# Entry 0's queries in one load: three chunks of a fused attention and feed-forward kernel are loaded and turned together

## The chip, the cores and the metric

The kernel runs on one core of a Trainium2 chip. The metric is device time in microseconds (us) of one execution; several executions are timed and their median is given. A separate execution was taken by the hardware profiler, and all durations below are from that one.

The core has five engines with a queue each: PE multiplies matrices and writes to PSUM, ACT evaluates functions and copies, DVE does elementwise work, POOL does elementwise work and issues most of the loads, SP issues the stores and the transposing transfers. Each works in its own order and waits for the others through semaphores. 16 DMA engines move the data.

## The reference

Eight batch entries, eight heads, 576 tokens, head size 64. Attention has no softmax: the scores are scaled, multiplied by a decay that depends on the distance of the two tokens, and multiplied with the values. The result, heads side by side, goes through a feed-forward layer with 512 inputs and 2048 hidden units.

```python
scores = scale * np.matmul(q, k.transpose(0, 1, 3, 2))
gamma = 1.0 - 2.0 ** (-5.0 - np.arange(H))
rel = pos[:, None] - pos[None, :]
Dmat = np.where(rel >= 0, gamma[:, None, None] ** rel[None, :, :], 0.0)
attn_out = np.matmul(scores * Dmat[None], v)
x = attn_out.transpose(0, 2, 1, 3).reshape(B * S, H * D)
h = x @ w_in
out = (h * (1.0 / (1.0 + np.exp(-1.702 * h)))) @ w_out
```

## The kernel before

**Two halves on one PE queue.** The attention makes `xT`, the input of the feed-forward layer with the 512 features on partitions and tokens along the row. The feed-forward layer takes 512 tokens at a time: `hidden` (L732) multiplies `w_in` with `xT` and ACT puts the result through the activation into `gT`; `project` (L765) multiplies `gT` with `w_out`. The attention of the entries 1 to 7 is cut into 21 bursts (L587) that are placed between the products of the feed-forward layer. Only entry 0 has no such products to lie between: the first feed-forward products need its 384 first tokens. Its attention is written out by hand, from L852 on, and is called the front here.

**The front, chunk by chunk.** Entry 0 has five chunks, four of 128 tokens and one of 64. For a chunk n of the first four, the steps are

- `transposes` (L405): PE turns the chunk's queries and keys, four products of 128x128 each with the identity matrix, so that the head dimension comes onto the partitions. They go to a PSUM bank, and `evac_t` (L416) copies queries and keys in one ACT instruction of 128x1024 to `qk`.
- `intra` (L537): eight products make the scores (L431) in two PSUM banks, and DVE multiplies them with the mask (L441) into `sm`.
- `values` (L444): eight products with the values (L454); eight that add to a running state of keys and values (L467); from chunk 1 on, eight that multiply the chunk's queries with the state of the chunks before it (L482).
- `evac_z` (L503): ACT copies the state to `zq` for the next chunk. `evac_o` (L514): DVE multiplies the outputs with the query's decay into `xT`.

Between these steps `fill` (L828) issues products of zeros, 23 in all, which nobody reads. After the outputs of chunk 2 the first four `hidden_part` (L838) start with the columns 0 to 384, and chunk 3 is finished among them. From there on PE has feed-forward products.

**PSUM.** There are eight banks: `S` is two banks for scores, `O` and `Z` one each for outputs and state, `W` one for turned operands, `H0`, `H1` and `U` the three of `psB`. The scores of chunk 1 use `H0` and `H1` (`intra(1, 1)`), those of the chunks 0, 2 and 3 use `S`. Each bank (or pair) has a key, and an instruction of another engine on the same key waits.

**Loads.** Queries and values of chunk 0 come by SP in 32-bit form and are converted by DVE. All other loads are issued by POOL in the order of the code (L808 to L824) and are converted to bf16 on the way. A load of a chunk (L219) has eight heads by 128 tokens, 1024 packets, each 64 numbers. Its packets carry 256 B in memory and 128 B in the on-chip buffer. Before chunk 3's queries and keys come those of the chunks 1 and 2 and their values. POOL then issues two quarter-loads of `w_in` (512 packets of 512 B written), and multiplies the values of the chunks 1 and 2 with their factors (L390) before it issues the remaining loads. From the 23rd of these loads on (weights not counted), `pace` (L206) lets a load wait for the sixth before it.

The order of instructions is that of the calls; a recorder (`Rec`) keeps for each key who wrote and read it and makes the waits. The buffer `st_q` has three slots of five chunks; entry 0 uses slot 0, entry 2 is the first to use slot 2.

## Time and profile before

| | |
|---|---|
| median of 3 runs | 300.31 us (299.10 to 302.96) |
| the profiled execution | 298.93 us, of it 297.1 us from the first to the last instruction |
| PE busy | 291.1 us, 98% of the span |
| ACT, DVE, POOL busy | 125.9, 123.1, 151.6 us |
| first feed-forward product of the front (L843) | 17.12 us after the span's start |

The span is counted from the first instruction; all times of single instructions are counted from there too. A row of the timeline gives an instruction's start, its duration (for several in a row, from the first start to the last end), its engine, line and operands, how many there are, and in brackets the idle time of the engine before it with what ended it. PE overlaps its products, so the time that eight products take from PE is the distance to the next start, not the sum of their durations.

### The profile page before, as it was taken

The page shows a single profiled execution, that of the slowest core. Times are in us where ns is not written, and L with a number is a line of the kernel's source. Part 1 is how long each engine was busy: PE and PEld are TensorE (multiplying, and loading weights), DVE is VectorE, ACT ScalarE, POOL GpSimd, SP SyncE. Part 2 cuts the span into 40 slices and gives each one's busy share as a digit, 9 for nine tenths or more (in the row PEclk, how much of TensorE's full clock was granted, in tenths as well). Part 3 has the DMA queues.
Part 4 walks back from the last instruction along what each step waited for, and adds up shares of the span by engine and source line. Part 5 has one row for each costly group of instructions (what it writes and reads, how often), then busy time and mean ns, then how long its engine had stood idle before and what let it go on. Part 6 is the DMA issues. An engine that isn't in the chain of part 4 may idle for free.

```text
span 297.1 us, 7697 instructions
## 1 busy us (share of the span) xinstructions
PE 291.1 (98%) x3399; PEld 148.5 (50%) x3399; DVE 123.1 (41%) x221; ACT 125.9 (42%) x208; POOL 151.6 (51%) x205
## 2 busy tenths in 40 slices
PE   7799999999999999999999999999999999999996
PEld 3464455848544444544454445545454445444444
DVE  7769475454445435532615324245326504000012
ACT  6658426617256313540355045503660275026600
POOL 8975979989959887568984797000000000000000
PEclk9999999999999999999999999999999999999999
DMA  9999999999999999999999999904820200030012
GB/s 133 156 186 190 173 171 165 188 131 140 182 140 143 183 143 175 194 130 134 154 218 124 114 188 162 85 2 108 170 38 2 107 37 2 0 108 35 0 50 93
DMA packets 154850, 36.04 MB, mean 121 GB/s; under 512 B 145472, under 2 KB 150336, under 8 KB 154816
## 3 DMA queue, kind: packets, MB, share of 16 engines
q0 software_dynamic: 116304, 18.10, 94.1%
q1 hardware_dynamic: 38512, 17.44, 32.6%
q8 instruction: 27, 0.44, 0.6%
q14 instruction: 7, 0.06, 0.1%
HBM read 36.70 MB, written 9.44 MB: 155 GB/s over the span
## 4 chain that ended last, share of the span: by engine, by line
PE 94%; POOL 2%; DMA 2%; issue 0%; DVE 0%; POOLq 0%
PE psB L765 40%; PE psB L732 36%; PE psB L749 5%; PE psA L627 2%; DMA st_k<-in_k_dram 2%; PE psA L599 2%; PE psA L641 2%; PE psA L615 1%; PE psA L765 1%; PE psA L791 1%; PE psB L843 1%; PE psA L411 1%; POOL st_k L219 1%; POOL st_q L219 1%; POOL st_v L219 1%
## 5 line engine op out<-in xcount | busy, mean ns | idle before, releaser
L765 PE MATMUL psB<-w_out_sb,gT 128*128 128x512 bf16 x544 | 122.0, 380 | 0.0
L732 PE MATMUL psB<-xT,w_in_sb 128*128 128x512 bf16 x492 | 108.9, 379 | 0.0
L737 ACT ACTIVATE gT<-psB 128x512 bf16<-128x512 f32 x123 | 73.5, 597 | 38.4 <-PE psB L732 38.1
L765 PEld LDWEIGHTS psB<-w_out_sb,gT 128*128 128x128 bf16 x544 | 51.8, 98 | 60.2 <-DVE sm L696 0.3
L732 PEld LDWEIGHTS psB<-xT,w_in_sb 128*128 128x128 bf16 x492 | 47.5, 98 | 56.5
L685 DVE TENSOR_TENSOR xT<-psA,gq 128x768 bf16<-128x768 f32 x21 | 20.1, 958 | 115.3 <-PE psA L615 115.3
L232 POOL DMA_DIRECT2D st_k<-in_k_dram x70 | 52.5, 774 | 15.2 <-DMA st_k<-in_k_dram 10.9
L774 ACT ACTIVATE osb<-psB 128x512 f32<-128x512 f32 x31 | 18.5, 597 | 90.2 <-PE psB L765 86.8
L232 POOL DMA_DIRECT2D st_v<-in_v_dram x70 | 51.9, 767 | 5.7 <-DMA st_v<-in_v_dram 3.3
L219 POOL DMA_DIRECT2D st_q<-in_q_dram x39 | 34.8, 891 | 10.2 <-DMA st_q<-in_q_dram 7.6
L390 DVE TENSOR_TENSOR st_v<-st_v,vfac 128x512 bf16<-128x512 bf16 x36 | 23.3, 681 | 1.2 <-DMA st_v<-in_v_dram 1.2
L714 DVE TENSOR_TENSOR zacc<-zacc,psA 128x256 f32<-128x256 f32 x49 | 20.5, 419 | 6.9 <-PE psA L627 5.7
L696 DVE TENSOR_TENSOR sm<-psA,maskw 128x768 bf16<-128x768 f32 x21 | 19.9, 948 | 0.0
L749 PE MATMUL psB<-xT,w_in_sb 128*128 128x256 bf16 x128 | 15.0, 273 | 0.0
L777 DVE COPY osb<-psB 128x512 f32<-128x512 f32 x3 | 2.1, 692 | 29.7 <-PE psB L765 29.7
L749 PEld LDWEIGHTS psB<-xT,w_in_sb 128*128 128x128 bf16 x128 | 12.2, 98 | 1.7
L418 ACT ACTIVATE qk<-psA 128x1024 bf16<-128x1024 bf16 x8 | 8.2, 1022 | 9.8 <-PE psA L411 9.8
L599 PE MATMUL psA<-sm,st_v 64*64 64x64 bf16 x504 | 11.8, 195 | 0.3
L627 PE MATMUL psA<-st_v,st_k 64*64 64x64 bf16 x448 | 11.8, 199 | 0.0
L627 PEld LDWEIGHTS psA<-st_v,st_k 64*64 64x64 bf16 x448 | 7.5, 105 | 8.3 <-issue 7.8
L755 ACT ACTIVATE gT<-psB 128x512 bf16<-128x512 f32 x16 | 9.4, 599 | 5.0 <-PE psB L749 5.0
L615 PE MATMUL psA<-qk,zw 64*64 64x64 bf16 x448 | 11.1, 194 | 0.0
(103 smaller groups left out, 164.3 us busy)
## 6 DMA issues: line engine op xcount, KB each, us to landing
out_dram<-osb SPq DMA_DIRECT2D x35, 256.0 KB, 3.9
st_q<-in_q_dram POOLq DMA_DIRECT2D x31, 128.0 KB, 7.5
st_k<-in_k_dram POOLq DMA_DIRECT2D x57, 64.0 KB, 7.3
st_v<-in_v_dram POOLq DMA_DIRECT2D x57, 64.0 KB, 7.0
w_out_sb<-in_moe_w_out_dram POOLq DMA_DIRECT2D x4, 512.0 KB, 10.9
w_in_sb<-in_moe_w_in_dram POOLq DMA_DIRECT2D x3, 512.0 KB, 8.6
st_k<-in_k_dram POOLq DMA_DIRECT2D x4, 128.0 KB, 4.8
w_in_sb<-in_moe_w_in_dram POOLq DMA_DIRECT2D x2, 256.0 KB, 6.8
```

The source lines that it names most:

```text
L219: paced(R.op("POOL", lambda e, d=d, s=s: e.dma_start(d, s), w=[(nm, sl, c)], dma=(nm, sl, c), own=pace()))
L232: paced(R.op("POOL", lambda e: [e.dma_start(d, s) for d, s in parts], w=[(nm, sl, c)], dma=(nm, sl, c), parts=2, own=pace()))
L390: R.op(eng, lambda e: e.tensor_tensor(t, t, f, ALU.mult), r=[("vfac", min(b, 1))], w=[("v", sl, c)])
L627: i = e.matmul(psA[half(j), bank, off + 64 * t : off + 64 * t + 64], rows_of(st_k, m_in, g, u, h), rows_of(st_v, m_in, g, u, h), start=(t ...
L685: R.op("DVE", lambda e: e.tensor_tensor(xT[:, :, t0 : t0 + 192].rearrange("p (u j) n -> p u j n", u=2), psA[:, 2:4, 0:384].rearrange("p u ...
L696: R.op("DVE", lambda e: e.tensor_tensor(o, i, k, ALU.mult), r=["maskw"], w=[("sm", si(m))], ps=["S"])
L714: R.op("DVE", lambda e, to=to, src=src, was=was: e.tensor_tensor(to, was, src, ALU.add), r=[("zacc", (blk - 1) % 3)], w=[("zacc", blk)], p ...
L732: i = e.matmul(bank, w_in_sb[:, a, 128 * f : 128 * f + 128], xT[:, a, 512 * c : 512 * c + 512], start=(a == 0), stop=(a == 3))
L737: R.op("ACT", lambda e: e.activation(gT[c % 2][:, f, :], bank, AF.Gelu_apprx_sigmoid), w=[("gT", c % 2, f)], ps=[key])
L749: m = e.matmul(bank[:, 256 * i : 256 * i + 256], w_in_sb[:, a, 128 * (f + i) : 128 * (f + i) + 128], xT[:, a, a0 : a0 + 256], start=(a == ...
L765: i = e.matmul(bank, gT[c % 2][:, f, 128 * r : 128 * r + 128], w_out_sb[:, f, :], start=(f == 0), stop=(f == NF - 1))
L774: R.op("ACT", lambda e: e.activation(osb[m].ap(), bank, AF.Copy), w=[("osb", m)], ps=[key])
```

## The change

The queries of entry 0's chunks 1 to 3 are 384 tokens. They are loaded in one transfer `load_q4` in place of three. A partition takes four tokens that follow one another, and 96 partitions hold a head's 384. Four tokens of a head are 1024 B without a gap in memory, so that the load has 768 packets of 512 B written, where the three had 3072 of 128 B. They are put in slot 2 of `st_q`.

In this form a chunk's tokens are not on partitions of their own. PE turns all three chunks at once in `turn_q4`: for every pair of heads, every one of the four token positions and each head of the pair a product of 96 partitions by 64 columns with the 96x96 identity matrix, 32 products. They fill the banks `H0` and `H1`. `evac_q4(n)` copies the chunk n's queries from there to `qk`, 128x512 by ACT, and reads with a step of 96 numbers between neighbours so that the tokens come out in order. The keys of the chunks 1 to 3 are turned on their own (`turn_k`), four products and a copy of 128x512 each.

Since `H0` and `H1` are taken, the scores of chunk 1 go to `S`, and those of chunk 2 to `H0` and `H1`, after the copy of chunk 3's queries has left these banks. The outputs of chunk 2 are made and scaled ahead of chunk 3's scores, as before, without the products of zeros in between; 19 of the 23 products of zeros stay. POOL issues the values of chunk 3 and the second half-load of `w_in` ahead of its two multiplications. The threshold of `pace` is lowered by two, as there are two loads fewer.

```diff
+        q4 = st_q[0:96, 2, 0:4, :].rearrange("p c x -> p (c x)").rearrange("p (h x) -> p h x", h=H)
+        def load_q4():
+            s = q[0, :, 128:512, :].rearrange("h (p j) d -> p h (j d)", j=4)
+            paced(R.op("POOL", lambda e: e.dma_start(q4, s), w=q4_keys, dma=("q4",), own=pace()))
...
+        def turn_k(n, at=None):
...
+                for hp in range(HP):
+                    i = e.matmul(to[:, a, hp, :], t[:, sl, c, 128 * hp : 128 * hp + 128],
+                                 ident.ap(), is_transpose=True)
...
+            R.op("ACT", lambda e: e.activation(qk[n % NQK][:, a, :, :], to[:, a, :, :], AF.Copy),
+                 w=[("qk", n % NQK, a)], ps=[key])
...
+        psQ_keys = [("H", 0), ("H", 1)]
+        def turn_q4():
+            def fn(e):
+                for hp in range(HP):
+                    for j in range(4):
+                        for hh in range(2):
+                            i = e.matmul(psQ[half(hh), hp, 96 * j : 96 * j + 96],
+                                         q4[:, 2 * hp + hh, 64 * j : 64 * j + 64],
+                                         ident[0:96, 0:96], is_transpose=True)
+                return i
+            R.op("PE", fn, r=["ident"] + q4_keys, ps=psQ_keys)
+        def evac_q4(n, eng="ACT"):
+            i = psQ[:, :, 0:384].rearrange("p h (j t) -> p h t j", j=4)[:, :, 32 * n - 32 : 32 * n, :]
+            o = qk[n % NQK][:, 0, :, :].rearrange("p h (t j) -> p h t j", j=4)
+            if eng == "ACT":
+                R.op("ACT", lambda e: e.activation(o, i, AF.Copy), w=[("qk", n % NQK, 0)], ps=psQ_keys)
...
-        load(0, 1, "qk")
-        load(0, 2, "qk")
+        load(0, 1, "k")
+        load_q4()
+        load(0, 2, "k")
         load(0, 1, "v")
         load(0, 2, "v")
-        load(0, 3, "qk")
+        load(0, 3, "k")
         load_w_in(0, 1)
         load_w_in(1, 2)
+        load(0, 3, "v")
+        load_w_in(2, 4)
         scale_v(1, "POOL")
         scale_v(2, "POOL")
-        load(0, 3, "v")
-        load_w_in(2, 4)
...
         transposes(0)
         evac_t(0)
-        later_gq(2)
         constants_mask3()
         fill(4)
-        transposes(1, second)
-        evac_t(1, second)
+        turn_k(1, second)
+        later_gq(2)
         intra(0)
-        fill(4)
-        intra(1, 1)
-        transposes(2)
-        evac_t(2)
+        fill(2, (psV[:, 0, :], "O"))
+        turn_q4()
+        evac_q4(1)
         values(0, third[0])
+        turn_k(2)
+        evac_q4(2)
+        intra(1, 0)
         evac_z(0)
+        evac_q4(3)
         evac_o(0, third[0])
         later_gq(3)
         fill(2, second)
-        intra(2)
+        intra(2, 1)
         values(1, third[1])
         evac_z(1)
         evac_o(1, third[1])
-        fill(1)
-        transposes(3)
-        evac_t(3)
+        turn_k(3)
         values(2, third[0])
         evac_z(2)
         evac_o(2, third[0])
-        fill(1)
         gelu_table()
         intra(3)
```

## The prediction, made before the changed kernel ran

> **What bounds the kernel now.** First the page's busy times, then the chain of work that ended last in order of time, then who waited for whom, then the timeline of the first 20 us by engine. The page:
>
> ```profile
> PE 291.1 (98%) x3399; PEld 148.5 (50%) x3399; DVE 123.1 (41%) x221; ACT 125.9 (42%) x208; POOL 151.6 (51%) x205
> ```
>
> PE is busy for 291.1 of 297.1 us. The list of waits, for PE alone over the whole span, has three lines:
>
> ```profile
> PE psA L411 <- DMA st_k<-in_k_dram: 1.3, 1, 1.3
> PE psB L831 <- DVE lnh L270: 1.2, 1, 1.2
> PE psA L411 <- DVE mask L307: 0.3, 1, 0.3
> ```
>
> All three lie in the front. The busy share flatters the front, since fills count as busy; but from 17.12 us on PE has feed-forward products and the same query over 35 to 297 us shows no wait. The change touches nothing behind the front: the sequence of instructions of every engine is the same there. So the kernel gets faster or slower by what the first feed-forward product (L843) moves. The chain of work, cut to the front:
>
> ```profile
> 7.93 0.81 POOL st_q L219
> 8.74 6.04 DMA st_k<-in_k_dram
> 14.78 0.14 issue
> 14.91 0.61 PE psA L411 x8
> 15.52 0.34 PE psA L454 x8
> 15.87 0.12 PE psA L467 x8
> 15.99 0.36 PE psA L482 x8
> 16.35 0.02 issue
> 16.37 0.70 DVE xT L518
> 17.08 0.05 issue
> 17.12 2.12 PE psB L843 x12
> ```
>
> Read it from below: 17.12 is set by chunk 2's outputs (DVE 16.37 to 17.07), these by PE's work on chunk 2, and that stood in PE's queue behind the turning of chunk 3, which waited for chunk 3's keys: issued at 8.74, landed at 14.78, 6.04 us later. The other seven such loads of 1024 packets ahead of it took 4.5 to 4.7 us from issue to landing (k0 excepted, which met the early loads). Asked for this load alone, the source view gives 4.7/5.4/6.0 for a window that also has the queries before it: 6.0 is the exception.
>
> **The change, part by part.** I replay the front with durations of rows. Those that carry it:
>
> ```profile
> 10.32 0.40 PE L411 MATMUL psA<-ident,st_q 128*128 128x128 bf16 x4
> 10.55 0.39 PE L411 MATMUL psA<-ident,st_k 128*128 128x128 bf16 x4
> 10.87 0.41 PE L454 MATMUL psA<-sm,st_v 128*64 128x128 bf16 x8
> 11.12 0.29 PE L467 MATMUL psA<-st_v,st_k 128*64 128x64 bf16 x8
> ```
>
> From start to start: four turning products 0.22, eight products with values 0.25, eight for the state 0.23; further, by the same timeline, eight scores 0.34, eight inter-chunk products 0.34, a fill 0.216. A copy on ACT starts 0.2 after the end of its products; a DVE step starts 0.44 after the first of eight score products; after ACT or DVE, PE follows in 0.06. DVE masks in 1.23 and scales outputs in 0.68, 0.1 of it overlapped with the next.
>
> *When the new load lands.* Now k1 is issued at 3.55; with no q1 before it, at 2.65, and the new load at 3.55. Not shown: a load of 768 packets of 512 B by 96 partitions. Lower end: it takes what a small load takes, 4.5, and lands at 8.05. Upper end: the first quarter of `w_in`, packets of the same size, 6.6 after issue, so 10.15. For the value: between 6 and 10 us, 4668 small packets pass (1167 per us, 0.88 us a load); between 13 and 14.9 us, 655 packets of 512 B (345 per us), 2.2 us for 768; the two `w_in` quarters land 1.25 us apart (9.61 + 6.6 and 10.35 + 7.1), 1.9 us for 768. So 1.0 to 1.35 longer than a small load: it lands at **9.3** (9.05 to 9.4). The Trainium skill (DMA: Bandwidth & Descriptors, section Anatomy of one DMA) fits a load issued by POOL as 2.0 us plus its bytes at 436 GB/s; for 0.79 MB that is an estimate of 3.8 us, and the load would be there at 7.35, before PE is free for it; the sum would be the -0.8 of the third rival below. For a small load of 0.26 MB the same fit gives 2.6 against the 4.5 that all rows show, so I go by the rows.
>
> *The 32 products.* Not shown either. Lower end 0.031 us each: the products with values also write halves of 64 partitions in turn and take 0.25 for eight. Upper end 0.043: 0.055 of a full turning product by 96/128 columns, with no overlap of the halves. Taken: the middle, 0.037, 1.2 us. 9.35 to 10.55. PE is free from 9.0 (fill 6.99 to 7.86, turning of k1 0.22, scores(0) at 8.27 after the copy that ends at 8.21, two fills 0.43), so nothing of this is hidden: queued behind it are outputs(0), the turning of k2 and scores(1).
>
> *The copies.* Three ACT copies of 128x1024 go (1.02 each), six of 128x512 come. Contiguous, those take 0.60 (the activation L849, 128x512), 0.51 from start to start. With a step of 96 numbers in PSUM no row exists: lower end 0.51, upper end 0.92 as for 1024 numbers. Taken: 0.51, the nearest row by size. ACT: q1 10.75; k2 at 11.45 (PE: outputs(0) 10.55, state 10.8, turning k2 11.03 to 11.25); q2 11.96; `evac_z(0)` 12.47 (0.28); q3 12.75 to 13.35.
>
> *The bank.* scores(2) now wait for the copy of q3 to leave `H0` and `H1`: 13.41 instead of 12.06. This is the added wait. Queued behind it on PE: outputs(1), the turning of k3, outputs(2). Mask(1), 11.86 to 13.1, and outputs(0) on DVE end before mask(2) is due at 13.85, so DVE is not late. mask(2) ends at 15.08, outputs(2) begin at 15.15, their inter products at 15.63, DVE scales 16.08 to 16.77, and the first feed-forward product starts at **16.83** against 17.12.
>
> *The wait that goes.* k3's turn comes at 14.57, after outputs(1), and costs 0.22 ahead of outputs(2), which wait for mask(2) until 15.15 anyway. k3 is issued at 7.05 instead of 8.74, behind equal bytes; at the pace above it lands at 12.9, with the extra 1.5 of before at 14.4. So this wait is covered by 0.2 to 0.5 us even with a late piece; beyond 14.9 it would cost one for one. What is late next is the chain load, products, copies, bank.
>
> *POOL and the rest.* Two issues fewer are 1.75 us. The values' factors are applied from 11.2 on (they stood at 11.10), end 13.4, and are wanted at 13.75 and 15.15: nothing. v3 and `w_in` ahead of them go out 3.5 us earlier, but behind a busy DMA; `w_in` is wanted at 16.8, where its first quarter (16.2 before) is there. Four fills fewer (0.86) and 0.53 net on the turning products cost PE nothing that is on the path. Late loads, SP's queue and the pacing stay in step.
>
> Sum: 16.83 - 17.12 = -0.3 us. On the profiled execution 298.93 that is 298.6. The runs' median, 300.31, lies 1.4 above the profiled one, so the time to be expected of a median is 300.31 - 0.3 = **300.0**.
>
> **The rivals.**
>
> *The chain through the new load is longer* (slower than before). Place: load, products, six copies, bank. It decides against the change when the first feed-forward product passes 17.12, that is when the load lands after 9.6, or the strided copies take over 0.65 from start to start (the first has 0.19 of slack before the copy of k2 is due at 11.45, the second and third stand on the path in full). Price: at the upper ends, landing at 10.15 gives +0.85, copies of 0.92 give 0.22 + 0.41 + 0.41 = +1.0, products at 0.043 +0.2, together 2.05 above the forecast; a piece as late as k3's was, 1.5 in place of the 0.85, makes 2.7. That is 300.3 to 302.7, middle 301.3. For it: the slow landings of k3 and `w_in`. Against: the seven loads near the new place in time were all regular.
>
> *The clock.* PE's first eleven fills, 1.19 to 6.07, take 0.44 each; the four at 6.99 take 0.26 and less: PE starts at half speed. The change takes four fills away, and turning products take a larger part of PE's work: place, the stretch from 9 to 17 us; it decides once a stretch is too poor in other products. Between 13.6 and 17.0 us PE was busy for 2.08 of 3.4 us and the products at 17.12 still took 0.18 each (2.12 for twelve), so what was there was enough. If the front falls back to half speed for as long as at the start, 4.9 us, 2.4 us of work are lost: 302.4. The Trainium skill (TensorE: Matmul & The Clock Gate, Part 4) says that turning products do not count as work for the clock, which speaks against this change; by that rule the least busy stretch before would already have been poor, and the trace shows no fall.
>
> *The wait was the whole story* (more gain). If the load lands by 9.0, when PE is free (its lower end is 8.05), and the products take 0.031, every step behind comes 0.5 earlier and the first feed-forward product is at 16.35: -0.8, 299.5. Nothing above gives more, as the rest of the chain stays.
>
> *It does not do what it says:* k3 still comes late and PE waits for it again. With k3 at 16.0 the gain is gone and 0.8 lost: 301.1. The chain would name its load.
>
> **How the numbers follow.** Forecast (16.4 to 17.2): 0.6. Longer chain 0.22, clock 0.06, more gain 0.08, k3 late 0.04. All of these move the time by under 1%, less than the runs' own spread of 3.9 us around it, so the range is set by both: from 299.5 less 1.2 (the lowest run lies 1.2 under the median) to the longer chain's end at 302.7: 298.3 to 302.7, which leaves out an unlucky median. A change of 2%, 6 us, about what can be told from no change here, needs more than any rival gives: 0.02 faster, 0.03 slower.
>
> **What would show it.** The row of the 32 products: start (9.3) and distance to outputs(0) (1.2). The three strided copies' mean: 0.6 or more. PE's wait ahead of scores(2), on ACT, and DVE's mask(2) at 13.85. No wait of PE on `st_k`; instead one on the new load of `st_q`. First L843 product at 16.8, each 0.18. I am wrong if that product starts later than 17.2, or if the time moves without it.

## The result

| | kernel before | changed kernel |
|---|---|---|
| median | 299.99 us (299.10 to 302.96, 6 runs) | 303.80 us (302.99 to 304.78, 6 runs) |
| ratio | | 1.0118 [1.0068, 1.0167] |
| profiled execution | 298.93 us, span 297.1 | 303.15 us, span 301.4 |
| first feed-forward product of the front | 17.12 us | 17.99 us |

A second set of runs of the changed kernel gave 303.61 us against 299.70, ratio 1.0137 [1.0085, 1.0188]. The predicted time was 300.0 and the range ended at 302.7: the kernel is 3.8 us slower, and both signs of error that the prediction had named came true. The front is late, by 0.87 us instead of 0.3 us early; and the end moved by 4.3 us, so in this execution most of the loss arises behind the front. (Ratios leave out executions more than 1.5% above the fastest of their kernel; where a loss comes and goes from one execution to the next, as it will below, the median of all runs is therefore given beside the ratio.)

The page of the changed kernel, its line of busy times and one of its groups of instructions (the group's last column is the idle time of the engine just before these instructions and what ended it):

```profile
PE 290.5 (96%) x3415; PEld 147.7 (49%) x3415; DVE 123.0 (41%) x221; ACT 126.3 (42%) x211; POOL 150.4 (50%) x203
L775 PE MATMUL psB<-xT,w_in_sb 128*128 128x512 bf16 x492 | 109.1, 380 | 2.1 <-issue 2.1
```

PE has 3415 products, 16 more than before, and is busy for 0.6 us less, in a span that is 4.3 us longer: it stands still more. The second line is the feed-forward layer's `hidden` (L732 before), 2.1 us idle ahead of it with the releaser "issue", that is, nothing the profile shows. The list of waits, for PE alone over the whole span, with the first six of its eleven lines (total, times, longest):

```profile
PE psB L775 <- issue: 2.1, 1, 2.1
PE psB L437 <- DMA st_k<-in_k_dram: 1.3, 1, 1.3
PE psB L875 <- DVE lnh L277: 1.2, 1, 1.2
PE psB L474 <- ACT qk L463: 1.0, 1, 1.0
PE psB L453 <- DMA st_q<-in_q_dram: 0.8, 1, 0.8
PE psB L887 <- DVE xT L561: 0.5, 1, 0.5
```

Before, there were three lines, all in the front, and none behind it. Here the 2.1 us on "issue" are one single pause. The timeline of PE shows where:

```profile
95.60 0.28 PE L658 MATMUL psA<-qk,zw 64*64 64x64 bf16 x12
95.82 1.25 PE L775 MATMUL psB<-xT,w_in_sb 128*128 128x512 bf16 x5
99.14 1.04 PE L775 MATMUL psB<-xT,w_in_sb 128*128 128x512 bf16 x4 [2.07 <-issue]
```

Five large products after a group of small ones (the attention of a later entry, 96 products in 0.96 us), PE stops in the middle of a row of identical products whose operands are all there, and goes on 2.07 us later. The fifth large product starts at 96.69 and the sixth at 99.14, where 0.22 apart is usual. That is 2.2 of the 4.3 us; the front gives 0.9, and the rest comes in three steps of 0.4 to 0.7 us between 37 and 90 us, two of them with a short wait on "issue" (0.28 us up to 79.1 and 0.17 us up to 89.4).

The chain of work that ended last, cut to the front (start, duration, what), answers the prediction's replay:

```profile
2.73 0.82 POOL st_k L219
3.55 7.44 DMA st_q<-in_q_dram
10.99 0.04 issue
11.04 0.87 PE psB L453 x32
11.91 0.23 PE psA L497 x8
12.13 0.12 PE psA L510 x8
12.26 0.34 PE psA L437 x4
12.60 0.02 issue
12.62 0.60 ACT qk L441
13.22 0.49 ACT qk L463
13.71 0.28 ACT zq L548
13.98 0.50 ACT qk L463
14.48 0.05 issue
14.53 0.42 PE psB L474 x8
...
15.04 1.24 DVE sm L484
16.28 0.04 issue
16.32 0.41 PE psA L497 x8
...
17.25 0.70 DVE xT L561
17.95 0.04 issue
17.99 1.15 PE psB L887 x6
```

It is the predicted chain, link by link: load, products, copies, bank, mask, outputs, scaling. It starts 1.7 us late, since the new load took 7.44 us and landed at 10.99 instead of 9.3. From landing to the first feed-forward product it takes 7.0 us; the prediction had 7.5.

A last view: the issues of transfers between 2 and 18 us, with the median time to landing in the last column. First the kernel before, then the changed one:

```profile
w_in_sb<-in_moe_w_in_dram POOLq DMA_DIRECT2D x2, 256.0 KB, 6.8
st_v<-in_v_dram POOLq DMA_DIRECT2D x3, 128.0 KB, 4.7
```

```profile
w_in_sb<-in_moe_w_in_dram POOLq DMA_DIRECT2D x2, 256.0 KB, 8.2
st_q<-in_q_dram POOLq DMA_DIRECT2D x1, 384.0 KB, 7.4
st_v<-in_v_dram POOLq DMA_DIRECT2D x3, 128.0 KB, 7.5
```

The loads of the values are the same instructions in both kernels, and issued earlier in the second; yet they take 7.5 us at the median instead of 4.7. So the new load is not only late itself, its neighbours are late with it. Each load lands in 16 pieces. In the trace of the changed kernel, chunk 1's keys, issued at 2.65, ahead of the new load, have 15 pieces by 6.61 and the last at 8.96; the new load itself has 14 by 9.31 and the last two at 10.71 and 10.99.

### The profile page after: what moved, and what is told of

Its sections match the earlier page's. It is cut to its first block, busy times and chain, and to the rows that moved or that the text cites. A ratio compares the mean times of both kernels' runs of the same rounds, so it can differ in the third digit from the quotient of the medians.

```text
span 301.4 us, 7729 instructions
## 1 busy us (share of the span) xinstructions
PE 290.5 (96%) x3415; PEld 147.7 (49%) x3415; DVE 123.0 (41%) x221; ACT 126.3 (42%) x211; POOL 150.4 (50%) x203
## 4 chain that ended last, share of the span: by engine, by line
PE 91%; DVE 3%; DMA 2%; issue 1%; POOL 1%; ACT 1%; POOLq 0%; DVEq 0%
PE psB L808 38%; PE psB L775 36%; PE psB L792 5%; DMA st_q<-in_q_dram 2%; PE psA L670 2%; PE psA L642 2%; PE psA L684 1%; PE psA L658 1%; PE psA L834 1%; PE psB L887 1%; PE psA L808 1%; POOL st_k L219 1%; PE psA L418 1%; DVE gT L344 1%; DVE sm L484 0%
## 5 line engine op out<-in xcount | busy, mean ns | idle before, releaser
L817 ACT ACTIVATE osb<-psB 128x512 f32<-128x512 f32 x31 | 18.5, 597 | 90.3 <-PE psB L808 89.8
L219 POOL DMA_DIRECT2D st_q<-in_q_dram x36 | 32.8, 910 | 10.5 <-DMA st_q<-in_q_dram 7.1
L642 PEld LDWEIGHTS psA<-sm,st_v 64*64 64x64 bf16 x504 | 7.8, 107 | 2.5 <-issue 1.7
```

The costliest lines, as they stand in the source:

```text
L219: paced(R.op("POOL", lambda e, d=d, s=s: e.dma_start(d, s), w=[(nm, sl, c)], dma=(nm, sl, c), own=pace()))
L642: i = e.matmul(psA[half(t), 2 + u, at : at + 64], rows_of(st_v, m_out, g, u, 4 * u + 2 * t + j), smw[si(m_out)][half(r), j, 2 * blk + t, : ...
```

## The experiments

Two questions were to be told apart: what the pause at the 97th us is, and what the large load costs in the front. Theory A for the pause: instructions reach PE in packets. The page counts 27 packets of 16 KB in the queue of instructions, and the trace 6880 records of PE in the kernel before, so about 255 to a packet; a product leaves two records, its weights and itself. One packet begins just when PE pauses (96.24 to 97.64 us). If PE runs out of instructions where a packet ends, then it matters how many products stand ahead of that place, and the change adds 16. Theory B: the moved transfers or the moved times of the front cause the pause.

**The changed kernel once more**, first a single execution, then a second set of runs.

> The changed kernel once more, for a second trace. In the first one the first feed-forward product starts 0.87 us later than before (17.99 against 17.12), chunk 1's keys land at 8.96 because one of the load's 16 pieces is 2.35 us behind the others, and PE stands still for 2.1 us at 96.9 with nothing that the profile shows as a cause (in all, the span is 4.3 us longer). If both are the change's own, the late piece of the keys' load (1.5 us or more behind) and a PE pause of about 2 us near 97 us are there again, and the span is 301 to 303. If the pause is chance, it is gone and the span is near 299.

> The changed kernel again, timed beside the next two on the same chip, as their yardstick: ratio to before 1.008 to 1.016. The queries' load lands at 10.7 to 11.0 again, with its slowest pieces 1.5 us or more behind the first. For PE's pause the earlier looks were split (2.1 us near 97 us in one of two), so either is possible here.

The single execution took 301.85 us (span 300.1), the second set 303.61 (303.08 to 306.37). The new load is late in both profiles, at 10.79 and 11.59; chunk 1's keys, issued ahead of it, are late only in the second (9.42, against 7.12 in the first, where the late piece that was expected is missing). In these two profiles the front is later still, first feed-forward product at 19.26 and 19.35. PE waited 1.8 and 0.9 us for the new load (the second time after 1.7 us for chunk 1's keys), and from then on its products ran slower; the granted clock was 0.52 to 0.63 between 12 and 16 us in the second. The long pause at the 97th us is in neither; the second has a shorter one, 1.1 us, from 80.0 to 81.3. So the loss is made up differently from one execution to the next.

**Sixteen products in the kernel before**, ahead of its `transposes(3)`, in a wait of PE:

```diff
+        def pad(e):
+            for _ in range(16):
+                i = e.matmul(psH[1][:, 0:64], idle[:, 0:128], idle[:, 0:64], start=True, stop=True)
+            return i
+        R.op("PE", pad, r=["idle"], ps=[("H", 1)])
```

> The kernel before with 16 small products of zeros (128x64) more, issued in the 1.3 us in which PE waits for chunk 3's keys, so that they cost nothing themselves (16 x 0.027 = 0.4 us). The changed kernel has 16 products more on PE than before (19 of 23 fills, 32 + 12 + 4 turning products in place of 32 in the front's first four chunks). Theory that PE's pause at 97 us comes from where PE's instruction stream is fetched, which those 16 products and their 16 weight loads move: this kernel gets a pause of 1 to 2.5 us somewhere between 60 and 130 us and is 1 to 3 us slower (ratio 1.003 to 1.009). Rival that the pause comes from the changed loads or is chance: no pause of more than 1 us, ratio 0.999 to 1.002.

302.63 us median of ten (299.24 to 306.13); the ratio of those that it keeps is 1.0031 [0.9987, 1.0074]. In the profile (303.85 us) the front is early, first feed-forward product at 16.11. And yet there is the pause: after the same 96 small products, two large ones, then 2.65 us of nothing.

```profile
94.27 0.59 PE L732 MATMUL psB<-xT,w_in_sb 128*128 128x512 bf16 x2 [0.16 <-issue]
97.51 1.48 PE L732 MATMUL psB<-xT,w_in_sb 128*128 128x512 bf16 x4 [2.65 <-issue]
```

The packet of instructions ran from 94.53 to 95.88. No load was touched here, which speaks against B, but the front's times moved.

The pause has a sequel. In the table of stretches (start and end in us, the busy time of each engine with its number of instructions, then the granted clock, the share of the DMA engines and GB/s) the clock falls to half behind it, and PE does 6 large products in 2 us where 11 are usual:

```profile
98.00:100.00 2.00, 2.00 (x6) 0.69 (x5) 1.03 (x2) 1.07 (x2) 1.49 (x3) 0.50 1.60 237
102.00:104.00 2.00, 2.00 (x11) 0.93 (x10) 0.00 (x0) 1.27 (x3) 1.92 (x3) 1.00 2.08 92
```

The trace has the clock at 0.5 from 97.9 to 101.4 us. These 3.4 us at half speed cost another 1.7 us, and the mean granted clock of this execution is 0.994. The pauses of 2.07 us in the changed kernel and of 2.47 and 1.67 us further below have no such fall.

**Sixty-four products in the changed kernel**, in its wait for chunk 1's keys (the same edit with 64, ahead of `turn_k(1)`).

> The changed kernel with 64 small products of zeros (128x64, 1.7 us) more, in the 1.9 us in which PE waits for chunk 1's keys. The start of the feed-forward products should not move by more than 0.2 us. Theory that the place of the instruction fetch makes the pause: moved by 128 instructions, the pause at 97 us goes or comes at another place with another length; if it goes, the kernel is about 2 us faster than the changed one (ratio to before 1.004 to 1.007). Rival that the changed loads make it: the pause stays at 97 us with 2.1 us, ratio 1.010 to 1.014.

302.97 us (301.26 to 306.01), ratio 1.0127 [1.0061, 1.0193]. There is no pause at the 97th us in the profile, but one of 0.9 us that ends at 84.6. The pause moved, as theory A says, and the time did not come down with it, as it had expected.

**Four loads of small packets for one of large ones.** The same data, the same order of work, 16 products more than before; each load has one of the four token positions, 768 packets of 128 B.

```diff
-            paced(R.op("POOL", lambda e: e.dma_start(q4, s), w=q4_keys, dma=("q4",), own=pace()))
+            paced(R.op("POOL", lambda e: [e.dma_start(q4[:, :, 64 * j : 64 * j + 64], s[:, :, 64 * j : 64 * j + 64])
+                                          for j in range(4)], w=q4_keys, dma=("q4",), parts=4, own=pace()))
```

> The changed kernel with its query load cut into four of 768 packets of 128 B, one for each token position; the 96 partitions, the 32 products and the order stay. Theory that packets of 512 B behind packets of 128 B make one or two of the 16 pieces late: chunk 1's keys land at 7.2 with all 16 pieces within 0.7 us; the queries' last part, with four issues of 0.8 us from 3.55 on, lands at 10.3 to 10.6; the late piece moves to chunk 3's keys, ahead of the first quarter of w_in. Rival that the load of 96 partitions or its source makes it: chunk 1's keys again come at 8.5 or later with one piece 1.5 us behind.

> The changed kernel with its query load in four of 768 packets of 128 B, timed. It has the changed kernel's 3415 products on PE. Theory that the large packets cost the front 0.5 to 1.3 us and the 16 more products another 2 to 3 us in most executions: 0.5 to 1.3 us under the changed kernel, but still slower than before, ratio 1.004 to 1.011. Rival that the large packets were the whole cause: ratio to before 0.998 to 1.003.

One execution took 299.62 us. The issues between 2 and 18 us in its profile:

```profile
st_q<-in_q_dram POOLq DMA_DIRECT2D x4, 96.0 KB, 4.3
st_v<-in_v_dram POOLq DMA_DIRECT2D x3, 128.0 KB, 4.6
```

The neighbours are back at 4.6 us at the median, the last query piece lands at 10.04 (9.82 in a second profile), and the first feed-forward product starts at 17.32 in both profiles. But the median of four executions is 303.00 (299.40 to 306.15), ratio 1.0133 [1.0068, 1.0197]. One execution would have told the wrong story: the loads' lateness is cured and the loss is still there in three of four executions. The profiled one (299.40) is the fourth, and it shows what goes well. The packet of instructions runs from 91.61 to 92.80, ahead of the small products, and PE goes through (the three others show a mean granted clock of 0.989 and 0.994):

```profile
93.83 0.28 PE L659 MATMUL psA<-qk,zw 64*64 64x64 bf16 x12
94.05 4.71 PE L776 MATMUL psB<-xT,w_in_sb 128*128 128x512 bf16 x21
```

**The same with 16 products in place of 32.** With the four loads laid out position by position, two heads' queries stand side by side and one product turns both, as in the transposes of the kernel before. PE has 3399 products, exactly as before.

```diff
-                        for hh in range(2):
-                            i = e.matmul(psQ[half(hh), hp, 96 * j : 96 * j + 96],
-                                         q4[:, 2 * hp + hh, 64 * j : 64 * j + 64],
-                                         ident[0:96, 0:96], is_transpose=True)
+                        i = e.matmul(psQ[:, hp, 96 * j : 96 * j + 96],
+                                     q4[:, j, 128 * hp : 128 * hp + 128],
+                                     ident[0:96, 0:96], is_transpose=True)
```

> As the one before, but the four loads put a token position's eight heads side by side, so that two heads are 128 columns in a row and 16 products of 96x128 do what 32 of 96x64 did. PE then has 3399 products, as the kernel before. The 16 products take 0.6 to 0.9 us in place of 0.7 to 0.9, so the front does not differ by more than 0.2 us. Theory of the fetch of PE's instructions: no pause over 1 us, and 2 to 3 us faster than the one before, ratio to before 0.999 to 1.004. Rival that the count of products does not matter: within 0.5 us of the one before.

299.56 us, ten executions between 299.18 and 300.16, ratio 0.9995 [0.9978, 1.0012]. The 16 products take PE 0.78 us where the 32 took 0.70, so those taken out had cost it nothing; and 3.4 us went with them.

**One quarter of `w_in` early in the kernel before**: `load_w_in(0, 1)` ahead of the queries and keys of chunk 2.

> The kernel before with its first quarter of w_in (512 packets of 512 B, 128 partitions) issued between the loads of chunks 1 and 2, at 4.4, in place of after chunk 3's. Theory that packets of 512 B behind packets of 128 B make pieces late, whatever the partitions: the quarter or the load ahead of it (chunk 1's keys, 8.02 before) has one or two pieces 1 us or more behind the other fourteen, and the loads of chunk 2, issued 0.8 us later than before, keep that lag and land 2 to 3.5 us later than before (queries 8.9 before). Rival that the form of the query load was the cause: all pieces within 0.8 us, and chunk 2's queries land 1.2 to 1.5 us later than before.

302.96 us in one execution (before: 299.70). Its packets are of 512 B as those of the new load, and it makes its neighbours late in the same way: chunk 1's queries, issued 1.8 us ahead of it, have the first piece at 6.19 and the last at 8.47; the three loads of queries take 6.4 us at the median, before 4.5. The front is 1.0 us late, PE waits 1.1 us for a later `w_in` load at the 23rd us, and 1.2 us for a transposing transfer at the 78th. So late pieces come with this load of large packets too, whatever it carries.

**Sixteen products where nothing else changes.** In the kernel before, two of the eleven fills that PE does ahead of its first product with data become 18 narrow ones:

```diff
-        fill(11)
+        fill(9)
+        narrow(18)
```

> The kernel before, with two of its first eleven fills (128x512, on TensorE before any load has landed) put as 18 narrow products of 128x64: TensorE issues 16 products more, which is what the change adds in all, and no load, no wait and no other engine is touched; the narrow products take 18 x 0.03 to 0.06 us = 0.5 to 1.1 us in place of 0.9 us. Theory A (the pause of TensorE at about 97 us comes where its instruction stream runs out in the stretch behind the 120 small products, and sixteen products more move that place into it): some executions pause 1 to 3 us, as with the sixteen products ahead of transposes(3): executions from 299.5 to 306 us, median 301.5 to 303. Theory B (the pause came from the moved transfers and the moved times of the front): the front is as before, so nothing pauses and the median is 299.3 to 300.2.

304.58 us median of ten (300.45 to 305.55), ratio 1.0124 [1.0081, 1.0167]. By the ratio this is as large as the whole loss of the change (1.0118 and 1.0137), and by the median larger than theory A's 301.5 to 303, from sixteen products of zeros that cost the front nothing: its first feed-forward product starts at 16.72, 0.4 early. The waits of PE begin with

```profile
PE psB L732 <- issue: 1.7, 1, 1.7
```

and the timeline shows it three large products behind the small ones:

```profile
95.50 0.82 PE L732 MATMUL psB<-xT,w_in_sb 128*128 128x512 bf16 x3
97.99 0.81 PE L732 MATMUL psB<-xT,w_in_sb 128*128 128x512 bf16 x3 [1.67 <-issue]
```

So the pause comes without theory B's causes. (The expectation speaks of 120 small products; by the timeline there are 96.)

The profiled execution, 302.66 us, is one of the three that kept the granted clock 1.00 (300.45 to 302.66 us). The seven others took 304.29 to 305.55, and each shows a mean of 0.994, as the one with the half clock behind its pause did. None of the seven was profiled, so that the clock fell behind a pause in them too is likely, not shown.

**A whole packet more.** If 255 records are a packet, 128 products more put every packet's end where it was. In the kernel before, fills are put as more and narrower ones until PE has 3527 products; in the changed kernel 112 are added to its 16, the same 3527.

```diff
-        fill(11)
+        fill(5)
+        narrow(50)
...
-        fill(4)
+        narrow(32)
...
-        fill(2, second)
+        narrow(16, second)
...
-        fill(1)
+        narrow(8)
```

> The kernel before, with fills of 512 columns put as more numerous narrow products of 128x64 in the same places, 128 products more in all. A product leaves two records on TensorE (weights and product), so these are 256 records, and between two 16 KB packets of the instruction queue some 250 records of TensorE are counted: the stream is moved by one whole packet. Theory A: the places where packets end stand against the small products as before, no pause, 299.3 to 300.5 us, although 128 products are added. A theory in which each added product costs something, or in which any longer stream pauses: 302 us or more, as with 16 and with 64 products.

> The changed kernel (16 products more than before) with 112 more as narrow products of 128x64, in place of fills and in TensorE's wait for chunk 1's keys: again 128 more than before in all, one whole packet; the query load of 512-byte packets and the order of the work stay. Theory A: the pauses of 1.1 to 2.5 us go, and what is left is the late front (0.9 to 2.3 us) with the 0.5 to 0.9 us that grow between 45 and 55 us: 300.9 to 302.2 us. Theory B (the late load and its transfers are the cause of the pauses too): 303 to 304.5 us as the changed kernel has.

The kernel before with 128 more: 300.51 us, ratio 1.0012 [0.9985, 1.0039]. The changed kernel with 112 more: 300.91 us, ratio 1.0037 [1.0010, 1.0063], nine of ten executions from 299.96 to 302.12. Adding 16 products costs 4.6 us, adding 128 costs 0.6, which can't be told from nothing; and the changed kernel with 112 products that do nothing is 2.7 to 2.9 us faster than in its two sets without them. The page of both counts one packet more:

```profile
q8 instruction: 28, 0.46, 0.7%
```

In the profile of the changed kernel with 112 more PE goes on behind the small products as it did before the change. First the kernel before (the view ends at 97), then this one:

```profile
93.27 0.28 PE L615 MATMUL psA<-qk,zw 64*64 64x64 bf16 x12
93.49 3.84 PE L732 MATMUL psB<-xT,w_in_sb 128*128 128x512 bf16 x17
```

```profile
95.44 3.84 PE L775 MATMUL psB<-xT,w_in_sb 128*128 128x512 bf16 x17
```

**The query load as two loads of 256-byte packets.**

> The changed kernel with its query load put as two loads of 256-byte packets (two tokens each) in place of one of 512. If the late pieces come with packets larger than the neighbours' 128 bytes and grow with them, the keys of chunk 1 land between the 7.3 us of the form with 128-byte packets and the 7.1 to 9.4 us of the form with 512, the last query piece at 10 to 10.8 us, and the following loads end 0.5 to 1.5 us behind their fifteenth piece. If it is only the one large load as such (0.79 MB in one issue), they are regular as with 128-byte packets.

303.05 us in one execution, with a pause of 2.47 us five large products behind the small ones; the packet ran from 95.67 to 97.18. The loads lie between the other two forms: chunk 1's keys by 7.26, the last query piece at 9.86, the following loads 0.8 to 1.0 us from first piece to last, the values' loads 5.7 us at the median (4.6 with packets of 128 B, 7.5 with 512). The first feed-forward product starts at 16.87, the earliest of all changed forms. So the lateness grows with the size of the packets. The size of an issue grows with it here (96, 192 and 384 KB), and only the early quarter of `w_in`, 256 KB in packets of 512 B, speaks for the packets; the one large issue alone is not needed for it.

**Other numbers of added products.** In the kernel before, 32, 64 and 96 more, by the same edits of the fills.

> The kernel before with 32 products more: four of the first eleven fills put as 36 narrow products. Reading of the pause (request 128 products ahead): TensorE holds one packet of 128 products in hand and asks for the next when it begins the last one; the 120 small products behind the 94th us take 1 us, so the stock lasts longest where the request falls inside them (the kernel before: 20 products behind them, 5 us in hand) and shortest where it falls just ahead of them (16 more: 3 to 5 products behind them, 2.6 us in hand, against 2.7 us and more that a packet takes from its start until TensorE goes on). With 32 more the request falls some 20 large products ahead of the small ones, 4 to 5 us in hand: no pause there, 299.5 to 300.8 us, unless another group of small products is hit. If every addition that isn't a whole packet hurts, 302.5 us or more, as with 16 and 64.

> The kernel before with 64 products more (fills put as narrow products, in the same places). By the same reading the place by the 94th us is out of danger; the changed kernel with 64 more (80 against before) had a pause of 0.9 us at the 83rd us, so another group may be hit: 299.5 to 301.5 us. If every addition that isn't a whole packet hurts, 302.5 us or more.

> The kernel before with 96 products more, in the same way: 299.5 to 301.5 us by the request's place, 302.5 or more if every addition that isn't a whole packet hurts. Of 32, 64 and 96 at least one is expected at or under the kernel before.

| products more | median, us | ratio |
|---|---|---|
| 16 (fills) | 304.58 | 1.0124 [1.0081, 1.0167] |
| 32 | 298.98, seven of ten up to 299.82, three from 303.82 | 0.9976 [0.9953, 0.9999] |
| 64 | 299.85 | 1.0016 [0.9985, 1.0046] |
| 96 | 298.89 | 0.9979 [0.9957, 1.0001] |
| 128 | 300.51 | 1.0012 [0.9985, 1.0039] |

An addition that is no whole packet doesn't hurt as such. Sixteen hurt; 32 hurt in three executions of ten, which the ratio leaves out and which have mean granted clocks of 0.989 and 0.994; none of them was profiled. With 64 the profile (301.26 us) has a pause of 0.8 us on "issue" that ends at 60.3, a wait of 1.9 us for a `w_in` load that ends at 23.0, and a front of 16.36.

**Small packets and a whole packet more**, to split the rest.

> The changed kernel with its query load as four loads of 128-byte packets and with 112 narrow products more (128 more than before in all): neither the late pieces nor the moved packet. Theory: the front is 0.3 us late as in the two profiles of that load, no pause: 299.6 to 300.6 us, so that against the same kernel with the large packets (300.9) the load's own share is 0.5 to 1.0 us. If the order of the work itself costs, 301 us or more.

300.91 us, ratio 1.0053 [1.0026, 1.0079]: the same as with the large packets, where 0.5 to 1.0 less was expected. The chain of work says why the split fails. It runs through the keys of chunk 2:

```profile
6.61 5.51 DMA st_k<-in_k_dram
12.12 0.05 issue
12.16 0.41 PE psA L438 x4
```

Of their 16 pieces 15 had landed by 10.81 and the last at 12.12, where all were there by 10.91 in the timed form without the added products; PE waits 0.7 us for them, and the first feed-forward product is at 17.97, not 17.32. The 72 narrow products push the turning of chunk 1's keys from 7.83 to 8.87, but the queries are turned at 10.09, right after they have landed (10.03), so that alone costs nothing. Late pieces hit this form too, then: its loads of values take 5.3 us at the median, not 4.6.

**The best number for both kernels.** The kernel before with 96 more again, and the changed kernel with 80 more (also 3495 products). In the wait for chunk 1's keys it has 36 narrow products in place of four fills, not 72; they end at 7.86, 0.5 us after the keys have landed.

> The kernel before with 96 products more (the same kernel as with 96 in the runs ahead of this one, 298.89 us there), to tell whether it beats the kernel before: 298.6 to 299.3 us and a ratio whose interval lies under 1, if the request's place is worth half a microsecond to the kernel before too; 299.5 or more if the gain was scatter.

> The changed kernel with 80 narrow products more in place of fills (96 more than the kernel before in all, none of them in TensorE's wait for chunk 1's keys), to be held against the kernel before with 96 more: both then have as many products, and the difference is what the change itself costs. By the late front alone (0.9 to 2.3 us in three profiles): 299.8 to 301.3 us. If the changed order loses behind the front whatever the place of the request, 302.5 us or more.

The kernel before with 96 more: 299.66 us, ratio 0.9990 [0.9967, 1.0012]. So its gain in the first set was scatter, and no version here is shown to beat the kernel before (the interval with 32 more lies under 1 only without its three long executions). The changed kernel: 301.96 us (299.12 to 306.30), ratio 1.0030 [0.9998, 1.0061]. The profiled one, 300.16, has no pause and a front of 17.95. Seven of twelve lie between 301.9 and 306.3, over the end of the expected range (301.3). Four of the seven have a mean granted clock of 0.978 to 0.989, three have 1.00; where they lose, no profile shows. The kernel before with as many products has no such executions (298.84 to 301.46). So the number of products alone doesn't decide it: the changed order or its load has a part in it that no run here separates.

## Why the prediction was wrong

**The step that failed first: "The change touches nothing behind the front".** From it followed that the kernel "gets faster or slower by what the first feed-forward product (L843) moves". Behind the front the order of instructions is the same, as the step says, and what it concludes from this is wrong: sixteen products more move every later instruction of PE against the ends of its packets. Taken together, the runs with 16 (in the fills, or the change's own) and with 128 products more, in both kernels, show that this is worth 2.7 to 4.6 us by the medians and 2.4 to 3.4 by the ratios. The sixteen ahead of `transposes(3)`, whose pauses come and go, give 2.9 by the median and 0.9, not clear of noise, by the ratio.

What the profiles show of the pause is first its place. In the five profiles that have such waits and a record of every product, PE waits on "issue" behind the front eleven times, the short waits of 0.17 us and more included. Each time 1473, 1985, 2241 or 2497 of PE's records lie ahead of the wait: always 193 more than a multiple of 256. So the packets end there, and a packet is 256 records, 128 products. (The traces with 16 ahead of `transposes(3)` and with 64 more in the changed kernel lack the records of some products and can't be counted.) Sixteen products more move each of these ends by 32 records through PE's work; 128 more move it by one whole packet.

The second is how late the packet was. The 256 records from 2241 to 2497 hold the 96 small products, and they last 7.6 us in the kernel before (89.98 to 97.60) and 7.5 in the changed one (89.42 to 96.91, where the next product was due). So the work in hand did not shrink. The next packet began 3.8 us after record 2241 in the kernel before (93.76) and 6.8 us after it in the changed one (96.24). In the execution with small packets in which nothing paused (299.40) it was 3.9 us; with 16 products more in the fills 6.2, and with 256-byte packets 7.1, and both paused. The reading behind the runs with 32 to 96 products more, that the stock is shortest where the request falls just ahead of the small products, is not borne out by these numbers.

How long a packet takes from its beginning until PE goes on can be read off every pause on "issue" of over 0.4 us:

```
kernel                              packet          pause            packet's end to going on
changed                             96.24 -  97.64  96.69 -  99.14   1.50
changed, second set                 78.49 -  79.64  80.01 -  81.26   1.62
changed, 64 more                    82.09 -  83.05  83.53 -  84.64   1.59
changed, 256-byte packets           75.50 -  76.81  77.44 -  78.18   1.37
changed, 256-byte packets           95.67 -  97.18  95.97 -  98.81   1.63
before, 16 ahead of transposes(3)   84.98 -  85.94  86.84 -  87.52   1.58
before, 16 ahead of transposes(3)   94.53 -  95.88  94.48 -  97.51   1.63
before, 16 in the fills             75.63 -  76.75  77.48 -  78.27   1.52
before, 16 in the fills             86.41 -  87.62  88.42 -  89.10   1.48
before, 16 in the fills             95.25 -  96.46  95.94 -  97.99   1.53
before, 64 more                     57.82 -  58.72  59.37 -  60.32   1.60
```

(The packets' times are those of their entries in the queue of instructions; a pause is from the start of the product ahead of it to the start of the next.) Eleven times of eleven PE goes on 1.4 to 1.6 us after a packet has ended, and the packet takes 0.9 to 1.5 itself, 2.5 to 3.1 together. By these times the packet that began 3.8 us behind record 2241 was there 1.1 us before PE needed it, and the one that began 6.8 us behind it came 2.2 us too late. Why a packet begins later when the ends of packets are moved by 32 records is open: the other transfers of that time take some 6 to 9 us from issue to landing in both kernels, so delays are no wonder, but they do not set the two apart.

The Trainium skill (Runtime: NRT & Kernel Launch, section Instruction fetch mechanics) has a sequencer fetch blocks of 16 KiB, 256 instructions, by a DMA queue of its own while it executes the block before; the 256 records to a packet and the one packet more with 128 products agree with that. It also calls the cost of crossing a block mostly hidden, and gives PE room for 2048 instructions; here crossing one took up to 3.0 us from one product's start to the next (94.48 to 97.51), and in the profiles of both kernels each packet of the first 130 us begins while PE works on the 256 records just ahead of it, so that one packet is in hand and not eight; in this the measurement decides against the page. It would have been the rule to weigh against this change.

**The second: "it lands at 9.3 (9.05 to 9.4)".** It landed at 10.99, 10.79, 11.59, 10.95, 11.22 and 10.95 in six profiles, all above the upper end of 10.15. The rate was about right: by 9.4, the end of the narrow range, 11 to 14 of the 16 pieces had landed. What was missing are the late pieces. They had been seen, in chunk 3's keys and the first `w_in` quarters, and the step "6.0 is the exception" put them aside. Only its size was exceptional: in eight profiles of the kernel before with its loads as they were, chunk 3's keys, just ahead of the first 512-byte load, took 4.7 to 6.2 us, over 5.0 in six of them, and the early `w_in` makes the loads around its new place late. The rival "The chain through the new load is longer" had this mechanism and its point of decision, a landing after 9.6. Its price of 1.5 us for a late piece was about right too (the landings are 1.5 to 2.3 after the 9.3); but it stood in a rival with a chance of 0.22 and not in the sum. The sign "no wait of PE on `st_k`" failed as well: PE waited 1.3 us for chunk 1's keys, whose last piece landed at 8.96, and this was hidden only because the new load came later still.

**Terms that were mis-sized to the other side.** The 32 products: 0.70 us to the next start, 0.022 each, below the lower end of 0.031; the forecast had 1.2. The strided copies, 0.59 to 0.62 long, follow in 0.5, as taken. The bank: scores(2) waited 1.0 us on ACT's third copy, as said, until 14.53. Chunk 3's keys (14.39) were turned at 15.67 and covered. With these, the chain behind the load is 0.5 shorter than forecast.

**The base of the comparison.** The wait of 1.3 us on chunk 3's keys, which the change was to take away, is itself a matter of one execution. In seven other profiles of the kernel before with products of zeros added, whose loads are the same, the first feed-forward product starts at 16.11, 16.72, 15.74, 16.36, 16.25, 16.53 and 17.36 us, beside the 17.12 of the one that was read; its front was among the late ones. Against the mean of these eight numbers, 16.5, six changed fronts with 512-byte packets (17.99, 19.26, 19.35, 18.09, 18.23, 17.95; mean 18.5) are 2.0 us late, not 0.9.

**The clock.** The rival asked for a fall to half speed because fills go. In two of six profiles with the large load PE did slow down, at waits for it; the first feed-forward product is 1.3 us later in these. Whether the fills taken away have a part in it was not tried. In the other four the front kept the granted clock 1.00. With sixteen products ahead of `transposes(3)` it fell behind a pause at the 97th us, a place that the rival did not name.

**What remains of the change itself**, when packets end where they did: 300.91 against 299.95, 1.0 us (ratio 1.0037 [1.0010, 1.0063]). The front of its profile, 18.23, is 1.1 us later than the 17.12 of the kernel before and 1.7 later than the mean of 16.5. What part of that is the large load could not be split.

## What to carry to other kernels

An engine whose queue is full of small products can run out of instructions: 96 products of 64x64 pass in under a microsecond, and the next packet of instructions needs 2.5 us and more from its beginning until the engine goes on. A wait on "issue" in the middle of a row of like instructions, beside an entry of the instruction queue that ends 1.4 to 1.6 us before it is over, is the sign, and so are waits that lie a multiple of 256 records apart; a handful of harmless instructions ahead of it, or taken away, tells whether it is that, and 128 products more should bring the old time back, as they did in the kernel before (300.51 against 299.95). An edit in one place of a long unrolled kernel should be timed against the same edit with such padding before its loss, or its gain, is put down to what it does. And where a load of large packets is put among loads of small ones, price the last of its 16 pieces, and of its neighbours', not the mean rate.

## What the runs showed that was not expected

- A load of 512-byte packets can make pieces of loads late that were issued up to 1.8 us ahead of it (chunk 1's keys: 15 of 16 pieces by 6.61, the last at 8.96; late in three of six profiles), and those behind it: 7.5 us to landing at the median instead of 4.7; with 256-byte packets 5.7, with 128-byte packets 4.6, and 5.3 in a third profile. The Trainium skill (DMA: Bandwidth & Descriptors, section Latency and other measured facts) says that two of the sixteen DMA engines are usually slower than the others; one or two late pieces of sixteen, as in the first profile of the changed kernel, agree with that (in others three or more are late), but the trace doesn't name the engine of a piece.
- Sixteen products of zeros at the start make a kernel of 300 us slower by 4.6 us (ratio 1.0124), and 128 do not. Where PE ran out of instructions, the number of its records up to there was 193 more than a multiple of 256 each time.
- PE went to a granted clock of 0.5 to 0.6 in the front after waits of 1.7 and 0.9 us close together, and kept 1.00 after waits of 1.3 and 0.8. One wait of 1.8 us slowed it in one profile and not in another. Behind a pause of 2.65 us it went to 0.5 for 3.4 us, behind one of 2.47 it did not.
- Turning a block of 96x64 costs 0.022 us, less than half of the 0.055 of one of 128x128, and one of 96x128 costs 0.049; and reading PSUM with a step of 96 numbers costs ACT nothing (0.59 to 0.62 us for 128x512, as in a row).
